# Cached attention on one core: K loaded by four heads of a batch, and the scores' matmul reading K^T in V's order of keys

## The chip, the core and the metric

The kernel runs on one core of one Trainium2 chip. A core has five engines with their own instruction streams, which wait for each other through semaphores: TensorE (PE: matmuls and transposes; its weight loads are listed as PEld), VectorE (DVE), ScalarE (ACT), GpSimd (POOL) and SyncE (SP), which here only issues loads. Sixteen DMA engines move data between the chip's memory and SBUF, the on-chip memory of 128 partitions. TensorE writes into PSUM, eight banks of 2 KB per partition. The metric is the device time of one execution in microseconds (us).

## The reference

Two independent blocks, A and B, of the same shape are computed and put side by side. With `B, Sq, D = 16, 64, 640` and `H, Sk, Dh = 32, 512, 128`, in bf16:

```python
q = (x @ wq).reshape(B, Sq, H, Dh).transpose(0, 2, 1, 3)
scores = einsum("bhqd,bhkd->bhqk", q, k_cache) * (Dh ** -0.5)
p = softmax(scores, axis=-1)
o = einsum("bhqk,bhkd->bhqd", p, v_cache)
y = o.transpose(0, 2, 1, 3).reshape(B, Sq, H * Dh) @ wo
```

The caches of K and V are by far the largest inputs: 268 MB of the 291 MB that are read. Softmax and P x V don't care in which order the 512 keys stand, as long as P's columns and V's rows stand in the same one. Both versions use that freedom.

## The kernel before

**Tiling.** Two batches of 64 queries fill 128 partitions, so a *step* `g` is one head of two batches. A *macro step* `m` is two steps, and a *period* `k` is two macro steps, that is four heads of two batches. There are 512 steps, 256 macro steps and 128 periods: four passes (a block, half of its 32 heads) of eight batch pairs of 16 heads.

**What a period does**, by the names in the plan and the lines of their emitters:

- KX (L550, PE): 32 transposes turn a loaded K tile (`kn_ring`) into K^T in PSUM banks 6 and 7, 64 keys at a time; KE (L557, DVE) copies it into `ktp_ring`. Two of each per period.
- SM (L596, PE): the scores of a step: two matmuls of 512 columns, one per batch, in the left and the right half of the array (`tile_position`), into one of four PSUM banks. Four steps per period, at its beginning.
- MX (L605, DVE) takes the negated maximum, EX (L621, ACT) the exponential into `p_ring` with the row sum, RC2 (L627, DVE) the reciprocals of two row sums, NM (L635, POOL) multiplies P by them into `pn_ring`.
- TR2 (L644, PE) transposes the two P of a macro step, and TE2 (L651, DVE) or TA2 (L656, ACT) copies the result into `pT_ring`: ACT for even macro steps, DVE for odd ones. PV2 (L666, PE) multiplies V by it, OE4 (L673, ACT) copies the result, OP2 (L681, PE) multiplies it by 512 columns of wo, and OX (L691, PE), once in four periods, by the other 128. OVP, OXP, OVF and OXF move these sums on.
- QN (L567, PE) projects queries for later heads, except near the end, and QEN (L583, ACT) copies them. QJ and QZ do so at the start. XT (L776) transposes a piece of block B's x in eight of the periods.

These steps are pipelined over periods: a period's TR2 and PV2 work on the P of the period before.

**K and V in memory.** A V load (L761) takes one batch of four heads, 512 KB: partition `p` holds keys 4p to 4p+3 of each head, in rows of 1 KB. A K load (L764) takes two heads of two batches, also 512 KB: 64 partitions per head, each with eight keys per batch, in rows of 2 KB. So K^T stands with eight groups of 64 keys, and V wants four groups of 128. The scores keep K's order. NM changes it: it reads P as `(th tl pp)` and writes `(tl pp th)`, that is two elements apart, and the transposes that follow read `pn_ring` in V's order.

**What sets the order.** Each engine's instructions are ordered by templates (`PHASES`, four of them, from periods 0, 16, 112 and 126): an entry names a kind, an offset in macro steps, a step of the macro step, and a time in the period. `build_plan` lays them out and works out the waits between engines from what each operation reads and writes.

Loads are ordered and held back by a planned clock (lines 296 to 351). `us(t)` turns a position in macro steps into planned time with `STEP_US`. A load's key is its first use less `LEAD` (K and V; V of the odd batch less `LEAD` - 1 on its pair's first use) or `WLEAD` (weights), but not before its ring slot is free: nine slots of K (`NKB`), five pairs of V (`NVP`). Loads are taken in the order of their keys; the clock starts at `START_US`, never stands before a load's key, and moves on by `DMA_US` with each. SP then holds the load until TensorE has done the last instruction planned before the clock, or, if that is earlier, before the load's first use less `BEFORE` macro steps. A lead of so many macro steps below means how far before its first use a load is let go.

Of the kernel before, what the change touches and what calls it, by code (L numbers as in the profile page):

```python
# [9 lines left out]
ALU = mybir.AluOpType  # L10
# [5 lines left out]
class Cfg:  # L16
# [6 lines left out]
    LEAD = 4.68  # L23
    WLEAD = 4.56
    STEP_US = ((8, 39.85), (32, 17.16), (256, 3.11))
    DMA_US = dict(LDK=1.40, LDV=1.44, LDWQ=1.8, LDWO=1.8, LDX=1.3, LDXR=0.5)
    START_US = -168.79
    BEFORE = 1.75
# [17 lines left out]
          ("QEZ", 0, 1, 2.19), ("QEJ", 2, 0, 2.79), ("EX", 1, 0, 3.02), ("QEN", -6, 0, 3.12), ("TA2", -2, 0, 3.58),  # L46
          ("QEZ", 0, 2, 4.2), ("EX", 1, 1, 4.36), ("XTE", 8, 0, 4.4), ("QEZ", 0, 3, 4.6), ("QEZ", 0, 4, 4.7),
          ("OVP", -3, 0, 5.0), ("QEZ", 0, 5, 5.61), ("OXP", -3, 0, 5.75), ("QEZ", 0, 6, 5.9), ("QEZ", 0, 7, 6.3)),
# [10 lines left out]
          ("QEN", -6, 0, 3.35), ("TA2", -2, 0, 3.59), ("EX", 1, 1, 4.45), ("OXP", -3, 0, 4.84), ("OVP", -3, 0, 4.86),  # L59
          ("XTE", 0, 0, 4.88)),  # L60
         (("KE", 3, 0, 0.04), ("RC2", -1, 0, 0.64), ("MX", 0, 0, 0.87), ("MX", 0, 1, 1.32), ("MX", 1, 0, 1.41),
          ("MX", 1, 1, 1.55), ("KE", 2, 0, 2.37), ("RC2", 0, 0, 3.49), ("TE2", -1, 0, 4.58), ("OXF", -3, 0, 5.55),
          ("OVF", -3, 0, 5.65)),
# [9 lines left out]
          ("OXF", -3, 0, 5.48)),  # L73
# [39 lines left out]
def build_plan(dims, cfg):  # L113
# [72 lines left out]
    def make_op(kind, m, sub, ts):  # L186
# [50 lines left out]
        if kind == "MX2":  # L237
            return mk("dve", "MX2", m, [], [bank(2 + g0 % cfg.NS), bank(2 + g1 % cfg.NS), ("negmax", r0), ("negmax", r1)],
                      ts)
        if kind == "RC4":  # L240
            rs = [g % cfg.NR for g in range(4 * k, 4 * k + 4)]
            return mk("dve", "RC4", k, [("rowsum", r) for r in rs], [("recip", r) for r in rs], ts)
        if kind == "SM":
            return mk("pe", "SM", (m, sub), [qres(2 * m + sub), ("ktp", ktslot(m))], [bank(2 + (2 * m + sub) % cfg.NS)],
                      ts)
# [222 lines left out]
def mha_kernel(nc, blocks, out, cfg=None):  # L468
# [32 lines left out]
    with contextlib.ExitStack() as es:  # L501
# [9 lines left out]
        kn_ring = sb("kn_ring", [128, NKB, 2, 8 * DH], BF16)  # L511
# [31 lines left out]
        def em_KX(e, op):  # L543
            m = op.idx
            kt_ps = [ps[:, cfg.KTB[m % 2] + hs, :].bitcast(BF16) for hs in range(2)]
            first = last = None
            for t in range(16):
                for hs in range(2):
                    r = slice(64 * hs, 64 * hs + 64)
                    last = e.transpose(kt_ps[hs][:, 64 * t:64 * t + 64], kn_ring[r, m % NKB, t // 8, t % 8 * DH:(t % 8 + 1) * DH],  # L550
                                       ident[r, r])
                    first = first or last
            return first, last
# [35 lines left out]
        def em_SM(e, op):  # L589
            m, sub = op.idx  # L590
            g = 2 * m + sub
            q = qc_ring[:, qcell[g // G // PPQ, g % SPB, g // G % PPQ // (SPB // G)], :]
            kt = ktp_ring[:, ktslot(m)].rearrange("p (hs j s) -> p hs j s", hs=2, j=2)
            first = last = None
            for j in range(2):
                ins = e.matmul(s_bank(g)[64 * j:64 * j + 64, :], q[:, 64 * j:64 * j + 64],  # L596
                               kt[:, sub, j], start=True, stop=True, tile_position=(0, 64 * j))
                first = first or ins
                last = ins
            return first, last  # L600

        def em_MX(e, op):
# [3 lines left out]
            return ins, ins  # L606

        def em_MX2(e, op):
            r, b = 2 * op.idx % NR, S_BANK0 + 2 * op.idx % NS
            ins = e.reduce_max(negmax[:, r:r + 2], ps[:, b:b + 2, :], axis=AX.X, negate=True)  # L610
            return ins, ins

        def em_RC4(e, op):
            r = 4 * op.idx % NR
            ins = e.reciprocal(recip[:, r:r + 4], rowsum[:, r:r + 4])
# [14 lines left out]
        def em_NM(e, op):  # L630
            g = op.idx
            r = g % NR
            src = p_ring[:, g % NP, :].rearrange("q (th tl pp) -> q th tl pp", th=2, tl=4)
            dst = pn_ring[:, g % NPN, :].rearrange("q (tl pp th) -> q th tl pp", tl=4, th=2)
            ins = e.tensor_scalar(dst, src, recip[:, r:r + 1], 1.0, ALU.mult, ALU.mult)  # L635
# [118 lines left out]
        def em_LDKV(e, op):  # L754
            m = op.aux
            blk, bp, grp, ps_, hh0 = step_info(2 * m)
            h0 = (ps_ % NHALF) * HH + hh0
            if op.kind == "LDV":
                h0 -= h0 % G
                src = blocks[blk][2][2 * bp + m % 2, h0:h0 + G].rearrange("g (p t) d -> p g (t d)", p=128)  # L760
                ins = e.dma_start(v_ring[:, m // 2 % NVP, m % 2], src)  # L761
# [122 lines left out]
```

## Time and profile before

| | |
|---|---|
| Median of three runs | 857.67 us (855.37 to 857.76) |
| The profiled execution | 857.66 us, its span 855.9 us |
| PE busy | 805.9 us, 94% of the span |
| DVE, ACT, POOL busy | 726.6, 633.0, 418.0 us (85, 74, 49%) |
| Moved by DMA | 297.13 MB, mean 347 GB/s |
| K loads: packets, time to landing | 65,536 of 2 KB; 6.7 us (A), 6.4 us (B) |
| V loads: packets, time to landing | 131,072 of 1 KB; 6.6 us (A), 6.3 us (B) |
| Scores' matmuls (L596) | 1,024, 137.6 us busy |
| POOL's normalization (L635) | 512 of 846 ns |
| Copies of K^T (L557) | 256 of 1,218 ns |

A profile line of a group of instructions reads: line, engine, operation, output<-input with shapes, how many; then busy time and the mean of one in ns; then the idle time of that engine just before them and what ended most of it. A line of the chain reads: start, length, engine and line, how many. The chain is followed back from the last instruction, at each step to what released it, so its shares tell which engine the end waited for. A wait line reads: who waited, for whom, us in total, how many times, the longest. Matmuls overlap, and their ends are modelled, so the spacing of groups says more than the length of one.

### The profile page before, as it was taken

Reading aid. Unit: us, or ns where it says so; the run is one execution under the profiler, and the core shown is the slowest. Engines: PE = TensorE matmul, PEld = TensorE weight load, DVE = VectorE, ACT = ScalarE, POOL = GpSimd, SP = SyncE. Lnnn points to the kernel's source line nnn. Section 1 sums busy time; section 2 is a strip of 40 time slices with the busy share of each in tenths; the row PEclk is TensorE's granted clock in tenths of the full one; section 3 lists DMA queues with packets and bytes.
Section 4 is the critical chain, followed back from the end, with each engine's and each line's share of the span. In section 5 each row is a group of like instructions: output and inputs, shape, how many; then the busy total and the mean of one; then the engine's idle time right before and its main releaser. Section 6 shows DMA issues by size and latency. Waiting matters only on the chain.

```text
span 855.9 us, 38296 instructions
## 1 busy us (share of the span) xinstructions
PE 805.9 (94%) x16953; PEld 561.8 (66%) x17084; DVE 726.6 (85%) x1184; ACT 633.0 (74%) x1450; POOL 418.0 (49%) x518
## 2 busy tenths in 40 slices
PE   5999999999999999999999899999999999999987
PEld 3566666666666766766666666666676666666665
DVE  3588888898888899898898788988888889889995
ACT  2677787787787777777777777777877867767775
POOL 0344554545544554554554445555455545446554
DMA  8999999999999999999999999999999999999993
GB/s 266 321 368 367 357 352 328 358 352 346 356 363 354 355 364 366 359 368 369 366 354 368 316 355 364 360 358 362 355 363 364 364 360 370 346 307 350 368 352 115
DMA packets 232581, 297.13 MB, mean 347 GB/s; under 512 B 14304, under 2 KB 166880, under 8 KB 232416
## 3 DMA queue, kind: packets, MB, share of 16 engines
q1 hardware_dynamic: 230112, 292.06, 100.2%
q8 instruction: 133, 2.18, 1.1%
q10 hardware_dynamic: 2304, 2.62, 0.9%
q14 instruction: 32, 0.26, 0.1%
HBM read 290.72 MB, written 2.62 MB: 343 GB/s over the span
## 4 chain that ended last, share of the span: by engine, by line
PE 81%; DMA 9%; DVE 3%; issue 3%; ACT 2%; POOL 1%; SPq 1%; POOLq 0%; ACTq 0%; DVEq 0%
PE ps L550 15%; PE ps L567 14%; PE ps L666 14%; PE ps L596 13%; PE ps L644 11%; PE ps L681 11%; DMA v_ring<-in_B_v_cache_dram 6%; PE ps L691 3%; DMA v_ring<-in_A_v_cache_dram 3%; DVE ktp_ring L557 2%; DVE negmax L605 1%; POOL pn_ring L635 1%; ACT p_ring L621 1%; DMA wq_sb<-in_A_wq_dram 1%; ACT pT_ring L656 1%
## 5 line engine op out<-in xcount | busy, mean ns | idle before, releaser
L635 POOL TENSOR_SCALAR pn_ring<-p_ring,recip 128x512 bf16<-128x512 bf16 x512 | 417.4, 846 | 429.9 <-DVE recip L627 403.2
L621 ACT ACTIVATE p_ring<-ps,negmax 128x512 bf16<-128x512 f32 x512 | 350.0, 689 | 77.5 <-DVE negmax L605 74.3
L557 DVE COPY ktp_ring<-ps 128x2048 bf16<-128x2048 bf16 x256 | 311.9, 1218 | 78.6 <-PE ps L550 78.3
L605 DVE TENSOR_REDUCE negmax<-ps 128x1 f32<-128x512 f32 x512 | 320.6, 683 | 19.7 <-PE ps L596 12.6
L550 PEld LDWEIGHTS ps<-ident,kn_ring 64*128 64x128 bf16 x8192 | 135.8, 95 | 99.2 <-issue 58.8
L550 PE MATMUL ps<-ident,kn_ring 64*128 64x64 bf16 x8192 | 167.4, 191 | 5.3 <-DVE ktp_ring L557 2.6
L673 ACT ACTIVATE oT_ring<-ps 128x512 bf16<-128x512 f32 x128 | 76.4, 597 | 123.7 <-PE ps L666 123.7
L567 PE MATMUL ps<-xT_sb,wq_sb 128*128 128x512 bf16 (+2 forms) x544 | 135.7, 376 | 26.8 <-issue 18.3
L666 PE MATMUL ps<-pT_ring,v_ring 128*128 128x64 bf16 x4096 | 142.7, 193 | 7.4 <-DMA v_ring<-in_B_v_cache_dram 4.1
L644 PEld LDWEIGHTS ps<-ident,pn_ring 128*128 128x128 bf16 x2048 | 124.9, 98 | 34.8 <-ACT p_ring L621 3.4
L644 PE MATMUL ps<-ident,pn_ring 128*128 128x128 bf16 x2048 | 137.4, 219 | 1.7 <-POOL pn_ring L635 1.2
L596 PE MATMUL ps<-ktp_ring,qc_ring 128*64 128x512 bf16 x1024 | 137.6, 387 | 1.2 <-issue 1.1
L666 PEld LDWEIGHTS ps<-pT_ring,v_ring 128*128 128x128 bf16 x4096 | 127.4, 98 | 15.9 <-DMA v_ring<-in_B_v_cache_dram 5.3
L681 PE MATMUL ps<-wo_sb,oT_ring 128*128 128x512 bf16 x497 | 132.1, 379 | 5.0 <-ACT pT_ring L656 2.5
L656 ACT ACTIVATE pT_ring<-ps 128x1024 bf16<-128x1024 bf16 x128 | 132.6, 1036 | 0.6 <-PE ps L644 0.4
L621 ACT ACTIVATION_READ_ACCUMULATOR p_ring<-ps,negmax 128x1 f32 x512 | 105.2, 206 | 0.0
L567 PEld LDWEIGHTS ps<-xT_sb,wq_sb 128*128 128x128 bf16 x660 | 54.9, 99 | 62.8 <-DMA wq_sb<-in_A_wq_dram 7.7
L651 DVE COPY pT_ring<-ps 128x1024 bf16<-128x1024 bf16 x128 | 86.3, 674 | 6.9 <-PE ps L644 6.8
L583 ACT ACTIVATE qc_ring<-ps 128x512 bf16<-128x512 f32 (+1 forms) x129 | 77.1, 597 | 14.2 <-PE ps L567 14.2
L596 PEld LDWEIGHTS ps<-ktp_ring,qc_ring 128*64 128x64 bf16 x1024 | 47.3, 109 | 37.4 <-issue 5.0
L681 PEld LDWEIGHTS ps<-wo_sb,oT_ring 128*128 128x128 bf16 x512 | 43.4, 98 | 31.8 <-ACT pT_ring L656 4.6
L627 DVE RECIPROCAL recip<-rowsum 128x2 f32<-128x2 f32 x256 | 39.9, 156 | 9.1 <-ACT p_ring L621 9.1
(16 smaller groups left out, 109.1 us busy)
## 6 DMA issues: line engine op xcount, KB each, us to landing
kn_ring<-in_A_k_cache_dram SPq DMA_DIRECT2D x128, 512.0 KB, 6.7
v_ring<-in_A_v_cache_dram SPq DMA_DIRECT2D x128, 512.0 KB, 6.6
kn_ring<-in_B_k_cache_dram SPq DMA_DIRECT2D x128, 512.0 KB, 6.4
v_ring<-in_B_v_cache_dram SPq DMA_DIRECT2D x128, 512.0 KB, 6.3
wq_sb<-in_A_wq_dram SPq DMA_DIRECT2D x8, 640.0 KB, 6.6
wo_sb<-in_A_wo_dram SPq DMA_DIRECT2D x8, 640.0 KB, 6.8
wq_sb<-in_B_wq_dram SPq DMA_DIRECT2D x8, 640.0 KB, 6.4
wo_sb<-in_B_wo_dram SPq DMA_DIRECT2D x8, 640.0 KB, 7.4
```

The lines of the kernel that those rows point to most:

```text
L550: last = e.transpose(kt_ps[hs][:, 64 * t:64 * t + 64], kn_ring[r, m % NKB, t // 8, t % 8 * DH:(t % 8 + 1) * DH], ident[r, r])
L557: ins = e.tensor_copy(ktp_ring[:, ktslot(op.idx)], ps[:, b:b + 2, :].rearrange("p b s -> p (b s)").bitcast(BF16))
L567: last = e.matmul(dst[:, col:col + n], wq_sb[:, qslot(hh // G), kt, (hh % G) * DH:(hh % G + 1) * DH], xT_sb[:, kt, lo * 128:hi * 128], sta ...
L596: ins = e.matmul(s_bank(g)[64 * j:64 * j + 64, :], q[:, 64 * j:64 * j + 64], kt[:, sub, j], start=True, stop=True, tile_position=(0, 64 * j))
L605: ins = e.reduce_max(negmax[:, r:r + 1], s_bank(g), axis=AX.X, negate=True)
L621: ins = e.activation(p_ring[:, g % NP, :], s_bank(g), ACTF.Exp, bias=negmax[:, r:r + 1], scale=1.0, accum_out=rowsum[:, r:r + 1])
L635: ins = e.tensor_scalar(dst, src, recip[:, r:r + 1], 1.0, ALU.mult, ALU.mult)
L644: ins = e.transpose(pt_flat(m)[:, (4 * sub + t) * 128:(4 * sub + t + 1) * 128], pn_ring[:, g % NPN, t * 128:(t + 1) * 128], ident[:, :])
L651: ins = e.tensor_copy(pT_ring[:, m % NT].rearrange("p s t q -> p (s t q)"), pt_flat(m))
L656: ins = e.activation(pT_ring[:, m % NT].rearrange("p s t q -> p (s t q)"), pt_flat(m), ACTF.Copy)
L666: ins = e.matmul(qo_ps[:, col:col + 64], v_ring[:, m // 2 % NVP, j, 2 * (m % 2) + sub, t * DH:(t + 1) * DH], pT_ring[:, m % NT, sub, t, 64 ...
L681: ins = e.matmul(out_ps, oT_ring[:, m // 2 % NO, 2 * (m % 2) + sub, :], wo_sb[:, wslot(ps_, hh // G), hh % G, 0:N0], start=(hh == 0), stop ...
```

## The change

K is loaded as V is: four heads of one batch per macro step, the even macro step of a period the first batch of the pair, the odd one the second. A load is still 512 KB. A head now has 32 partitions with 16 keys each, in rows of 4 KB, and `kn_ring` is declared to match. KX does the same 32 transposes; a bank of K^T now holds two heads of one batch.

So the scores of every step need both K^T tiles of their period, one per batch. SM's matmul reads its 512 keys from `ktp_ring` through `(tl, s, th)`: four neighbours in the result stand 256 elements (512 bytes) apart in `ktp_ring`, the next four begin one element further on, and so on over 32; four such blocks make the 512. The scores, and P after them, come out in V's order, and NM reads and writes without a step.

The templates have other times, and with them some instructions another place: in the middle periods OP2 and OX stand between the two TR2, and on VectorE the fourth MX stands behind KE and RC2. The planned clock's constants differ: `LEAD`, `WLEAD`, `STEP_US`, `DMA_US` of K, `START_US` and `BEFORE`. Two kinds of operation that no template uses (MX2, RC4) are gone.

```diff
-    LEAD = 4.68
-    WLEAD = 4.56
-    STEP_US = ((8, 39.85), (32, 17.16), (256, 3.11))
-    DMA_US = dict(LDK=1.40, LDV=1.44, LDWQ=1.8, LDWO=1.8, LDX=1.3, LDXR=0.5)
-    START_US = -168.79
-    BEFORE = 1.75
+    LEAD = 4.99
+    WLEAD = 4.82
+    STEP_US = ((8, 43.5), (32, 3.92), (256, 3.1))
+    DMA_US = dict(LDK=1.36, LDV=1.44, LDWQ=1.8, LDWO=1.8, LDX=1.3, LDXR=0.5)
+    START_US = -319.64
+    BEFORE = 0.68
...
         (16,
-         (("SM", 0, 0, 0.0), ("SM", 0, 1, 0.21), ("SM", 1, 0, 0.43), ("SM", 1, 1, 0.64), ("KX", 2, 0, 1.42),
-          ("QN", -6, 0, 2.07), ("TR2", -2, 0, 2.96), ("TR2", -1, 0, 3.76), ("OP2", -4, 0, 3.83),
-          ("OP2", -3, 0, 3.98), ("XT", 0, 0, 4.35), ("OX", -3, 0, 4.75), ("KX", 5, 0, 4.88), ("PV2", -2, 0, 5.52),
-          ("PV2", -1, 0, 6.09)),
+         (("SM", 0, 0, 0.0), ("SM", 0, 1, 0.21), ("SM", 1, 0, 0.43), ("SM", 1, 1, 0.64), ("KX", 2, 0, 0.92),
+          ("QN", -6, 0, 2.17), ("TR2", -2, 0, 3.28), ("OP2", -4, 0, 3.43), ("OX", -3, 0, 3.76), ("TR2", -1, 0, 4.03),
+          ("OP2", -3, 0, 4.11), ("KX", 5, 0, 4.55), ("XT", 0, 0, 4.6), ("PV2", -2, 0, 5.55), ("PV2", -1, 0, 5.79)),
...
-         (("KE", 3, 0, 0.04), ("RC2", -1, 0, 0.64), ("MX", 0, 0, 0.87), ("MX", 0, 1, 1.32), ("MX", 1, 0, 1.41),
-          ("MX", 1, 1, 1.55), ("KE", 2, 0, 2.37), ("RC2", 0, 0, 3.49), ("TE2", -1, 0, 4.58), ("OXF", -3, 0, 5.55),
-          ("OVF", -3, 0, 5.65)),
+         (("KE", 3, 0, 0.23), ("RC2", -1, 0, 0.35), ("MX", 0, 0, 0.49), ("MX", 0, 1, 1.09), ("MX", 1, 0, 2.05),
+          ("KE", 2, 0, 3.29), ("RC2", 0, 0, 4.28), ("MX", 1, 1, 4.65), ("OXF", -3, 0, 5.26), ("TE2", -1, 0, 5.66),
+          ("OVF", -3, 0, 5.81)),
...
         if kind == "SM":
-            return mk("pe", "SM", (m, sub), [qres(2 * m + sub), ("ktp", ktslot(m))], [bank(2 + (2 * m + sub) % cfg.NS)],
-                      ts)
+            return mk("pe", "SM", (m, sub), [qres(2 * m + sub), ("ktp", ktslot(2 * k)), ("ktp", ktslot(2 * k + 1))],
+                      [bank(2 + (2 * m + sub) % cfg.NS)], ts)
...
-        kn_ring = sb("kn_ring", [128, NKB, 2, 8 * DH], BF16)
+        kn_ring = sb("kn_ring", [128, NKB, 16 * DH], BF16)
...
-                    last = e.transpose(kt_ps[hs][:, 64 * t:64 * t + 64], kn_ring[r, m % NKB, t // 8, t % 8 * DH:(t % 8 + 1) * DH],
-                                       ident[r, r])
+                    last = e.transpose(kt_ps[hs][:, 64 * t:64 * t + 64], kn_ring[r, m % NKB, t * DH:(t + 1) * DH],
+                                       ident[r, 64 * hs:64 * hs + 64])
...
-            kt = ktp_ring[:, ktslot(m)].rearrange("p (hs j s) -> p hs j s", hs=2, j=2)
+            hd = 2 * (m % 2) + sub
             first = last = None
             for j in range(2):
+                kt = ktp_ring[:, ktslot(m // 2 * 2 + j)].rearrange("p (hs th tl h s) -> p hs h tl s th", hs=2, th=4, tl=4, h=2)
                 ins = e.matmul(s_bank(g)[64 * j:64 * j + 64, :], q[:, 64 * j:64 * j + 64],
-                               kt[:, sub, j], start=True, stop=True, tile_position=(0, 64 * j))
+                               kt[:, hd // 2, hd % 2], start=True, stop=True, tile_position=(0, 64 * j))
...
-            src = p_ring[:, g % NP, :].rearrange("q (th tl pp) -> q th tl pp", th=2, tl=4)
-            dst = pn_ring[:, g % NPN, :].rearrange("q (tl pp th) -> q th tl pp", tl=4, th=2)
-            ins = e.tensor_scalar(dst, src, recip[:, r:r + 1], 1.0, ALU.mult, ALU.mult)
+            ins = e.tensor_scalar(pn_ring[:, g % NPN, :], p_ring[:, g % NP, :], recip[:, r:r + 1], 1.0, ALU.mult, ALU.mult)
...
-            blk, bp, grp, ps_, hh0 = step_info(2 * m)
+            blk, bp, grp, ps_, hh0 = step_info(2 * (m - m % 2))
             h0 = (ps_ % NHALF) * HH + hh0
+            src = blocks[blk][2 if op.kind == "LDV" else 1][2 * bp + m % 2, h0:h0 + G]
             if op.kind == "LDV":
-                h0 -= h0 % G
-                src = blocks[blk][2][2 * bp + m % 2, h0:h0 + G].rearrange("g (p t) d -> p g (t d)", p=128)
-                ins = e.dma_start(v_ring[:, m // 2 % NVP, m % 2], src)
+                ins = e.dma_start(v_ring[:, m // 2 % NVP, m % 2], src.rearrange("g (p t) d -> p g (t d)", p=128))
             else:
-                src = blocks[blk][1][2 * bp:2 * bp + 2, h0:h0 + 2].rearrange("j hs (p t) d -> (hs p) j (t d)", t=8)
-                ins = e.dma_start(kn_ring[:, m % NKB], src)
+                ins = e.dma_start(kn_ring[:, m % NKB], src.rearrange("h (p t) d -> (h p) (t d)", t=16))
```

More of the change, by code (lines that the diff above doesn't have):

```diff
@@ L39 @@
         (0,
[6 rows of a table removed]
-          ("QEZ", 0, 1, 2.19), ("QEJ", 2, 0, 2.79), ("EX", 1, 0, 3.02), ("QEN", -6, 0, 3.12), ("TA2", -2, 0, 3.58),
-          ("QEZ", 0, 2, 4.2), ("EX", 1, 1, 4.36), ("XTE", 8, 0, 4.4), ("QEZ", 0, 3, 4.6), ("QEZ", 0, 4, 4.7),
-          ("OVP", -3, 0, 5.0), ("QEZ", 0, 5, 5.61), ("OXP", -3, 0, 5.75), ("QEZ", 0, 6, 5.9), ("QEZ", 0, 7, 6.3)),
[10 rows of a table removed]
-          ("QEN", -6, 0, 3.35), ("TA2", -2, 0, 3.59), ("EX", 1, 1, 4.45), ("OXP", -3, 0, 4.84), ("OVP", -3, 0, 4.86),
-          ("XTE", 0, 0, 4.88)),
-         (("KE", 3, 0, 0.04), ("RC2", -1, 0, 0.64), ("MX", 0, 0, 0.87), ("MX", 0, 1, 1.32), ("MX", 1, 0, 1.41),
-          ("MX", 1, 1, 1.55), ("KE", 2, 0, 2.37), ("RC2", 0, 0, 3.49), ("TE2", -1, 0, 4.58), ("OXF", -3, 0, 5.55),
-          ("OVF", -3, 0, 5.65)),
[9 rows of a table removed]
-          ("OXF", -3, 0, 5.48)),
[11 rows of a table removed]
[6 rows of a table added]
+          ("QEZ", 0, 1, 2.63), ("EX", 1, 0, 3.46), ("QEN", -6, 0, 3.51), ("QEZ", 0, 2, 3.61), ("TA2", -2, 0, 3.61),
+          ("ST", -33, 0, 3.79), ("QEZ", 0, 3, 4.05), ("QEZ", 0, 4, 4.15), ("QEZ", 0, 5, 4.37), ("OVP", -3, 0, 4.63),
+          ("QEZ", 0, 6, 4.91), ("OXP", -3, 0, 5.07), ("EX", 1, 1, 5.29), ("XTE", 32, 0, 6.2), ("QEZ", 0, 7, 6.29)),
+         (("KE", 3, 0, 0.16), ("RC2", -1, 0, 0.49), ("MX", 0, 0, 1.09), ("OXF", 21, 0, 1.23), ("MX", 0, 1, 1.88),
+          ("MX", 1, 0, 2.26), ("KE", 2, 0, 2.77), ("RC2", 0, 0, 3.61), ("MX", 1, 1, 4.45), ("TE2", -1, 0, 4.74),
+          ("OVF", 31, 0, 5.52)),
[6 rows of a table added]
+          ("TA2", -2, 0, 4.54), ("EX", 1, 1, 4.81), ("OVP", -3, 0, 4.97), ("XTE", 0, 0, 5.08), ("OXP", -3, 0, 5.22),
+          ("ST", -9, 0, 6.24)),
+         (("KE", 3, 0, 0.23), ("RC2", -1, 0, 0.35), ("MX", 0, 0, 0.49), ("MX", 0, 1, 1.09), ("MX", 1, 0, 2.05),
+          ("KE", 2, 0, 3.29), ("RC2", 0, 0, 4.28), ("MX", 1, 1, 4.65), ("OXF", -3, 0, 5.26), ("TE2", -1, 0, 5.66),
+          ("OVF", -3, 0, 5.81)),
[9 rows of a table added]
+          ("OVF", -3, 0, 5.88)),
[11 rows of a table added]
     )
@@ L236, in make_op @@
             return mk("act", kind, idx, [], [bank(b)] + [("qc", c_) for c_ in cells], ts, aux=cells)
-        if kind == "MX2":
-            return mk("dve", "MX2", m, [], [bank(2 + g0 % cfg.NS), bank(2 + g1 % cfg.NS), ("negmax", r0), ("negmax", r1)],
-                      ts)
-        if kind == "RC4":
-            rs = [g % cfg.NR for g in range(4 * k, 4 * k + 4)]
-            return mk("dve", "RC4", k, [("rowsum", r) for r in rs], [("recip", r) for r in rs], ts)
         if kind == "SM":
-            return mk("pe", "SM", (m, sub), [qres(2 * m + sub), ("ktp", ktslot(m))], [bank(2 + (2 * m + sub) % cfg.NS)],
-                      ts)
+            return mk("pe", "SM", (m, sub), [qres(2 * m + sub), ("ktp", ktslot(2 * k)), ("ktp", ktslot(2 * k + 1))],
+                      [bank(2 + (2 * m + sub) % cfg.NS)], ts)
         if kind == "RC2":
@@ L605, in em_MX @@
             ins = e.reduce_max(negmax[:, r:r + 1], s_bank(g), axis=AX.X, negate=True)
[L606 to L615, printed above, removed]
             return ins, ins
@@ L785, in em_XTE @@
             return ins, ins
-        emitters = dict(KX=em_KX, KE=em_KE, QJ=em_Q, QEJ=em_QE, QZ=em_Q, QEZ=em_QE, QN=em_Q, QEN=em_QE, SM=em_SM, MX=em_MX, EX=em_EX, RC2=em_RC2, MX2=em_MX2, RC4=em_RC4,
+        emitters = dict(KX=em_KX, KE=em_KE, QJ=em_Q, QEJ=em_QE, QZ=em_Q, QEZ=em_QE, QN=em_Q, QEN=em_QE, SM=em_SM, MX=em_MX, EX=em_EX, RC2=em_RC2,
                         NM=em_NM, ND=em_NM, TR2=em_TR2, TE2=em_TE2, TA2=em_TA2, PV2=em_PV2, OE4=em_OE4, OP2=em_OP2, OX=em_OX, OXH=em_OX,
```

55 rows, old and new, of the table PHASES are left out of this document.

## The prediction

> **What bounds the kernel now.** I read the engine shares first, then the DMA queues, the chain that ended last, the chain between 300 and 400 us, and the waits on loads. Four lines of the page:
>
> ```profile
> PE 805.9 (94%) x16953; PEld 561.8 (66%) x17084; DVE 726.6 (85%) x1184; ACT 633.0 (74%) x1450; POOL 418.0 (49%) x518
> ...
> q1 hardware_dynamic: 230112, 292.06, 100.2%
> ...
> PE 81%; DMA 9%; DVE 3%; issue 3%; ACT 2%; POOL 1%; SPq 1%; POOLq 0%; ACTq 0%; DVEq 0%
> ...
> L635 POOL TENSOR_SCALAR pn_ring<-p_ring,recip 128x512 bf16<-128x512 bf16 x512 | 417.4, 846 | 429.9 <-DVE recip L627 403.2
> ```
>
> TensorE carries 81% of the chain, but the load queue is full as well. POOL's normalization waits for its input about as long as it works, and is 1% of the chain. Next, the chain inside 300 to 400 us (start, length, engine and line): one period of four heads.
>
> ```profile
> 305.82 0.98 PE ps L596 x8
> 306.80 0.57 PE ps L550 x32
> 307.53 1.03 PE ps L567 x4
> 308.56 0.89 PE ps L644 x16
> 309.45 0.86 PE ps L681 x4
> 310.32 0.57 PE ps L550 x32
> 310.89 1.04 PE ps L666 x32
> 311.93 0.98 PE ps L596 x8
> ```
>
> A period is 311.93 - 305.82 = 6.11 us of TensorE with no wait for another engine. The scores (L596) take 0.98 us: four pairs, 0.245 us each. I measured every period from score group to score group: most are 6.11 us, every fourth 7.00 (L691 adds 0.89), and the eight with L776 have 0.28 more. Without the query projection (L567, absent in the last 13 periods) 5.08 would do. Of the 855.9 us, 15.6 lie before the first scores, 14.2 after the last score group starts, and 793.4 are such full periods; that leaves 32.7. Of these 12.6 belong to periods 0 to 3 (mostly extra projections), 14 to periods 4 to 112, 6 to the end, where VectorE is late. The 14 us are what a better load order could win; the waits show where half of it sits (who waited: us, times, longest):
>
> ```profile
> PEld ps L666 <- DMA v_ring<-in_B_v_cache_dram: 5.3, 9, 1.3
> ...
> PEld ps L666 <- DMA v_ring<-in_A_v_cache_dram: 2.4, 4, 1.3
> ```
>
> 7.7 us are waits of PV2 for V. The timeline of periods 67 and 68 shows two of them (start, length, then the idle time before and its releaser):
>
> ```profile
> 466.60 1.11 PE L666 MATMUL ps<-pT_ring,v_ring 128*128 128x64 bf16 x32 [1.16 <-DMA v_ring<-in_B_v_cache_dram]
> ...
> 473.79 1.11 PE L666 MATMUL ps<-pT_ring,v_ring 128*128 128x64 bf16 x32 [1.01 <-DMA v_ring<-in_B_v_cache_dram]
> ```
>
> **The change part by part.** *K's rows.* In the trace's packet records the median packet takes 46 ns for 1,024 bytes and 84 for 2,048: 38 ns per KB and 8 fixed. By that line 4,096 bytes take 160. K's 65,536 packets of 84 ns are 344 us of each of the 16 engines; 32,768 of 160 ns are 328. So 16 us, 1.9% of a queue that is 100% busy, come free. They shorten nothing while TensorE is the bound; they shorten waits for loads. From below the gain is nothing (K's queue time stays); above, it can't exceed the waits.
>
> *When loads are issued.* SP holds each load until TensorE reaches an instruction, chosen by the planner (lines 334 to 351). I worked its formula through for both sets of constants. Before, V's loads 73 and 137 are held until 1.75 half-periods (BEFORE) ahead of their PV2: 1.75 x 3.06 = 5.4 us, against a median landing of 6.3 to 6.6 us. That is about 1 us too late, which is the size of the waits in periods 37 and 69, where their PV2 runs. Loads 133 and 135 (periods 67 and 68) get 2.49 and 2.00. After, with LEAD 4.99, K at 1.36 and the lower BEFORE, loads 73, 133, 135 and 137 are released 2.30, 3.07, 2.67 and 2.32 half-periods ahead, at least 7.0 us; the mean lead of a V load in the middle of the run rises from 3.4 to 4.0. The shortest lead then exceeds the landing by 0.4 us. K's and V's rings are unchanged, and their reuse was counted. SP's issues stay 512, of 0.37 us each. If the queue got longer with the earlier issue, the landing would rise and the waits stay: at worst nothing is won. I take the 7.7 us as gone, and with them 1 us of short pauses without a named releaser beside them (0.56 and twice 0.19 us near 156 to 170 us): **-8.7 us**.
>
> *Scores with a step.* Each of the 1,024 matmuls reads its 512 columns in another order: the innermost four lie 512 bytes apart, where they were neighbours. Weights, columns and PSUM writes stay, which excludes a gain: 0 is the low end. No row shows TensorE reading its moving operand so. The only stepped stream here is POOL's own write, two elements apart: 846 ns for 512 against POOL's memsets of 102 ns (1 element) and 205 ns (128), which extrapolate to 519 ns. Taking 102 ns off each, that is 744 against 417, a factor of 1.8. On TensorE it would make 0.245 us into 0.44, +0.195 x 512 = **+100 us**, the high end, since TensorE has no cover. A nearer row: the chain's single 512-column matmul (L681) takes 0.215 us, and the score pair, two tiles each with a 512-column stream of its own, 0.245 us. So the reading side delivers two streams in nearly the time of one. That is the same engine, same memory, same operand; I therefore take 0, and keep the high end as a rival.
>
> [...]
>
> *Scores wait for both K^T tiles.* Every SM now needs the odd and the even macro step's KE. Both were already copied one period earlier: in the timeline from 414 us the later copy (KE 2) ended 4.1 us into its period, 2 us before the next scores can start. Slot 0 of ktp_ring is free for the next KE only after all four SMs, 0.5 us later, but that KE comes 1.5 us after them at the earliest. Cost 0; queued behind such a wait would be all of TensorE.
>
> *Normalization without a step.* 512 instructions on an engine that is half idle; TR2 reads the result one period later. Where POOL is on the chain (789, 805, and 843 to 848 us, some nine instructions), contiguous writes could save at most 0.33 us each, 3 us; at the low end nothing changes. I take 0, since reading and multiplying remain.
>
> *Order on the engines.* In the middle periods OP2 and OX move between the two TR2, and on VectorE the fourth maximum moves behind KE 2 and RC2. By the trace's durations the fourth maximum then ends 4.3 us into a period and TE2 at 4.95, while the PV2 that reads it starts at 5.6; the fourth EX started at 4.76 already before. Cover 0.5 to 0.6 us; with it gone the rest goes into each period. VectorE does some 5.9 of 6.11 us, so this is the thinnest cover. In the last 13 periods its chain is 3 x 0.63 + 1.13 + 0.60 + 0.60 + 0.07 + 1.12 + 0.07 = 5.48 us before and after. Cost 0, bounded by -2.5 (the delay at 737 to 757 us, where the period's plan changes, disappears) and +0.1 us per middle period, +10 us.
>
> Startup: first weights land at 7.65 us as before, and the order of the first three K copies is the same; 0, with 2 us either way.
>
> Sum: 857.66 us (the profiled execution; its span is 855.9, 1.8 lie around it; the median shown is 857.67, the same) - 8.7 = **849 us**.
>
> **The rivals.** *Half-rate scores (slower).* If the stepped read lets the array take only one of two streams at a time, a pair becomes two single matmuls, 2 x 0.215 = 0.43 us: +0.185 x 512 = 95 us. Load waits (8.7) and the end's VectorE delay (6) vanish under it: 857.7 + 95 - 15 = 938 us; with POOL's factor 943. For it: the only stepped row; against it: the pair's row. It decides from a pair of 0.262 us on, 17 ns more, where 512 x 17 ns eats the 8.7 us.
>
> *A partial loss.* Pairs 10 to 30% longer: +12.5 to +38 us, less the load waits: 861 to 887 us.
>
> *Nothing is won.* Loads issued earlier only queue longer, HBM or the queue being full (100.2%): V's waits stay and the time is 855.5 to 860. For it: busiest slices reach 370 GB/s and none more. The slice where the waits of period 67 begin moves 368. Against it: the loads that come late are those that the formula itself releases later than a landing ahead.
>
> *VectorE becomes late.* The moved maximum delays TE2 and so PV2 by 0.1 us in each of some 100 periods, +10, with the load waits gone: 858 to 870 us.
>
> **How the numbers follow.** As forecast: 0.56, own range 842 to 855 (the 8.7 us by half lost, or with POOL's 3 us and the 2.5 us won). Nothing won: 0.08. Partial loss 0.12, VectorE late 0.07, half rate 0.17. By the 0.3% (2.6 us) that a measurement of this kernel tells from no change: faster 0.56, same 0.08, slower 0.36. The range 841 to 887 holds all but the half rate, 0.83.
>
> **What the changed profile would show.** Right: L596's eight matmuls at 0.98 us in the chain, periods at 6.11 and 7.00, no PEld wait on v_ring over 0.3 us, q1's share near 98% with 32,768 packets fewer, POOL at 520 to 846 ns. Wrong: L596 at 1.1 to 1.8 us per group (stepped read), V waits with landings over 7 us (queue), or PE waits for pT_ring or ktp_ring in every period (order).

## The result, and the profile after

The changed kernel takes 1247.57 us (median of four runs, 1247.43 to 1248.33) against 856.52 us before (median of four): a ratio of 1.457 (95% interval 1.454 to 1.460). It is 391 us slower, where 849 us were forecast. The profiled execution took 1247.60 us, its span 1245.8.

The lines of the page after that answer to those shown of before:

```profile
PE 1208.2 (97%) x16942; PEld 570.7 (46%) x17084; DVE 770.9 (62%) x1184; ACT 675.2 (54%) x1450; POOL 350.4 (28%) x518
...
q1 hardware_dynamic: 197344, 292.06, 73.5%
...
PE 97%; issue 2%; ACT 0%; DMA 0%; DVE 0%; SPq 0%; ACTq 0%
PE ps L590 43%; PE ps L543 12%; PE ps L560 11%; PE ps L648 11%; PE ps L626 9%; PE ps L663 9%; PE ps L673 2%; DMA wq_sb<-in_A_wq_dram 0%; PE ps L756 0%; ACT pT_ring L638 0%; DVE ktp_ring L550 0%; ACT p_ring L605 0%; SPq L733 0%; ACT oT_ring L655 0%; DVE negmax L599 0%
...
L617 POOL TENSOR_SCALAR pn_ring<-p_ring,recip 128x512 bf16<-128x512 bf16 x512 | 349.7, 696 | 886.4 <-PE ps L626 556.0
L590 PE MATMUL ps<-ktp_ring,qc_ring 128*64 128x512 bf16 x1024 | 544.0, 1194 | 0.0
```

TensorE is now nearly the whole chain (97%), and the scores (L590; L596 before) are 43% of it, where they were 13%. Their group before read:

```profile
L596 PE MATMUL ps<-ktp_ring,qc_ring 128*64 128x512 bf16 x1024 | 137.6, 387 | 1.2 <-issue 1.1
```

The load queue, 100.2% busy before, is 73.5% busy. One period of the chain, with the PV2 just before it, from the window at 400 to 425 us:

```profile
405.24 1.04 PE ps L648 x32
406.28 4.14 PE ps L590 x8
410.42 0.57 PE ps L543 x32
410.99 0.16 issue
411.15 1.03 PE ps L560 x4
412.17 0.45 PE ps L626 x8
412.62 0.43 PE ps L663 x2
413.05 0.45 PE ps L626 x8
413.50 0.43 PE ps L663 x2
413.93 0.57 PE ps L543 x32
```

Every other step lasts as long as before. The group of eight score matmuls takes 4.14 us here instead of 0.98: a pair 1.035 us instead of 0.245, 2.0 ns for each column. Followed through the whole run, the chain's 128 such groups last between 4.07 and 4.40 us, 4.18 on average. That is 3.20 us more per period, 410 us over 128 periods. The kernel lost 391 us, so some 19 us of other time that the kernel before spent went away under the slower scores. The 7.7 us of waits for V are part of it, since no wait of TensorE for V is left; the rest was not traced to its places. The granted clock was 0.999.

### The profile page after: what moved, and what is told of

It reads as the page before. It is cut to its first block, busy times and chain, and to the rows that moved or that the text cites. A ratio compares the mean times of both kernels' runs of the same rounds, so it can differ in the third digit from the quotient of the medians.

```text
span 1245.8 us, 38217 instructions
## 1 busy us (share of the span) xinstructions
PE 1208.2 (97%) x16942; PEld 570.7 (46%) x17084; DVE 770.9 (62%) x1184; ACT 675.2 (54%) x1450; POOL 350.4 (28%) x518
## 3 DMA queue, kind: packets, MB, share of 16 engines
q1 hardware_dynamic: 197344, 292.06, 73.5%
## 4 chain that ended last, share of the span: by engine, by line
PE 97%; issue 2%; ACT 0%; DMA 0%; DVE 0%; SPq 0%; ACTq 0%
PE ps L590 43%; PE ps L543 12%; PE ps L560 11%; PE ps L648 11%; PE ps L626 9%; PE ps L663 9%; PE ps L673 2%; DMA wq_sb<-in_A_wq_dram 0%; PE ps L756 0%; ACT pT_ring L638 0%; DVE ktp_ring L550 0%; ACT p_ring L605 0%; SPq L733 0%; ACT oT_ring L655 0%; DVE negmax L599 0%
## 5 line engine op out<-in xcount | busy, mean ns | idle before, releaser
L617 POOL TENSOR_SCALAR pn_ring<-p_ring,recip 128x512 bf16<-128x512 bf16 x512 | 349.7, 696 | 886.4 <-PE ps L626 556.0
L590 PE MATMUL ps<-ktp_ring,qc_ring 128*64 128x512 bf16 x1024 | 544.0, 1194 | 0.0
L599 DVE TENSOR_REDUCE negmax<-ps 128x1 f32<-128x512 f32 x512 | 351.4, 687 | 202.6 <-PE ps L590 202.6
L590 PEld LDWEIGHTS ps<-ktp_ring,qc_ring 128*64 128x64 bf16 x1024 | 58.7, 122 | 239.4 <-issue 231.0
L626 PEld LDWEIGHTS ps<-ident,pn_ring 128*128 128x128 bf16 x2048 | 132.5, 98 | 48.3 <-issue 0.3
L626 PE MATMUL ps<-ident,pn_ring 128*128 128x128 bf16 x2048 | 153.6, 219 | 0.0
L663 PE MATMUL ps<-wo_sb,oT_ring 128*128 128x512 bf16 x470 | 143.4, 379 | 8.1 <-issue 4.6
L605 ACT ACTIVATION_READ_ACCUMULATOR p_ring<-ps,negmax 128x1 f32 x512 | 101.0, 197 | 0.0
L663 PEld LDWEIGHTS ps<-wo_sb,oT_ring 128*128 128x128 bf16 x512 | 38.3, 98 | 28.6 <-issue 23.3
```

Of the source, the lines that this page charges most:

```text
L599: ins = e.reduce_max(negmax[:, r:r + 1], s_bank(g), axis=AX.X, negate=True)
L605: ins = e.activation(p_ring[:, g % NP, :], s_bank(g), ACTF.Exp, bias=negmax[:, r:r + 1], scale=1.0, accum_out=rowsum[:, r:r + 1])
L617: ins = e.tensor_scalar(pn_ring[:, g % NPN, :], p_ring[:, g % NP, :], recip[:, r:r + 1], 1.0, ALU.mult, ALU.mult)
L626: ins = e.transpose(pt_flat(m)[:, (4 * sub + t) * 128:(4 * sub + t + 1) * 128], pn_ring[:, g % NPN, t * 128:(t + 1) * 128], ident[:, :])
L663: ins = e.matmul(out_ps, oT_ring[:, m // 2 % NO, 2 * (m % 2) + sub, :], wo_sb[:, wslot(ps_, hh // G), hh % G, 0:N0], start=(hh == 0), stop ...
```

## The experiments

**Theories.** S: a column costs about 2 ns (1.035 us over the changed kernel's 512 columns) whenever it lies in another line of 16 bytes of SBUF than the one before; at that price, an estimate, 256 changes of line come to 0.52 us a pair. D: the distance of 512 bytes, a large power of two, is at fault. Q: two stepped streams are served in turn. N: any innermost step but one element is slow. R: the loss isn't the read at all but the rows, the second K^T tile or the order.

**The change without the stepped read (e1).** K^T is read in runs of 32 neighbours, and POOL does the rest of the reordering:

```diff
-    ...rearrange("p (hs th tl h s) -> p hs h tl s th", hs=2, th=4, tl=4, h=2)
+    ...rearrange("p (hs t h s) -> p hs h t s", hs=2, t=16, h=2)
...
-            ins = e.tensor_scalar(pn_ring[:, g % NPN, :], p_ring[:, g % NP, :], recip[:, r:r + 1], 1.0, ALU.mult, ALU.mult)
+            src = p_ring[:, g % NP, :].rearrange("q (th tl s) -> q th tl s", th=4, tl=4)
+            dst = pn_ring[:, g % NPN, :].rearrange("q (tl s th) -> q th tl s", th=4, tl=4)
+            ins = e.tensor_scalar(dst, src, recip[:, r:r + 1], 1.0, ALU.mult, ALU.mult)
```

> Everything of the change is kept but the stepped read: the scores read K^T in runs of 32 neighbours, and the normalization on POOL brings P into V's order, writing four elements apart. If the whole loss is the stepped read: groups of eight score matmuls back at 0.98 us, periods at 6.11 us, 849 us as the prediction's sum had it without that term (842 to 855). If the loss is the 4 KB rows, the wait for both K^T tiles or the new order of instructions: near 1247 us. If POOL's wider step hurts: 846 ns rises above 1,200 ns and waits of TR2 for pn_ring appear, 860 us and more.

Measured: 898.12 us, ratio 1.049 (1.047 to 1.052). Groups of this kernel:

```profile
L619 POOL TENSOR_SCALAR pn_ring<-p_ring,recip 128x512 bf16<-128x512 bf16 x512 | 680.6, 1415 | 204.5 <-DVE recip L611 183.2 <-PE ps L628 20.3
L590 PE MATMUL ps<-ktp_ring,qc_ring 128*64 128x512 bf16 x1024 | 136.7, 387 | 0.7 <-issue 0.7
```

The scores are back at 136.7 us (137.6 before), so R falls: rows, both K^T tiles and order together are not the 391 us. The 42 us that remain go with POOL: writing four elements apart takes it 1,415 ns, against 846 at two and 696 without a step, and it is 29% of this kernel's chain. The kernel with a step of 4 bytes further down (e11) bears this out. It has the rows, both tiles and the order too, but no step on POOL, and takes 857.48 us. With the planned clock's old constants (e2):

> As the kernel with runs of 32, but the loads' planned clock has the constants of before. If the earlier release of V's loads is what takes its waits away: the waits of PV2 for V stay near 7 us and the time is 856 to 858 us. If the cheaper 4 KB rows do it by themselves: 849 to 851 us.

Measured: 901.23 us, ratio 1.054 (1.052 to 1.056). POOL's longer time hides what the expectation asked for; the waits of PV2 for V were 3.3 us there, and none with the new constants.

**What makes the read slow.** Six kernels (e5, e6, e7, e8, e11 and e12, with their expectations below in this order) change only the order in which the score matmul reads, for instance e6:

```diff
-    ...rearrange("p (hs th tl h s) -> p hs h tl s th", hs=2, th=4, tl=4, h=2)   [:, hd // 2, hd % 2]
+    ...rearrange("p (i o) -> p o i", o=8)[:, 2 * hd:2 * hd + 2]                  # step of 16 bytes
```

> Of each pair of score matmuls only the one of the second batch reads with the step of 512 bytes; the first reads 512 neighbours (so the first batch's scores have their keys in another order, and its output is not the reference's). If each stream is slowed by itself: the pair still takes 1.03 us, time near 1247 us. If two stepped streams are served in turn and one costs half: pair 0.52 us, 843 + 512 x 0.275 = 984 us.

> Score matmuls read 512 columns with an innermost step of 8 elements, 16 bytes (the keys are mixed over heads, so the output is not the reference's). If a column costs 2.0 ns whenever it lies in another 16-byte line than the one before: pair 1.03 us, 1247 us. If the 512 bytes, a large power of two, are at fault: pair 0.245 us, 843 to 855 us.

> Innermost step of 4 elements, 8 bytes: two columns in each 16-byte line (keys mixed over heads, output not the reference's). [...] If any innermost step other than one element is slow: 1.03 us, 1247 us.

> Score matmuls read runs of two neighbours, the next run 128 bytes on (keys out of V's order, output not the reference's). [...] If what counts is the distance or the number of jumps of 128 bytes and more: between 0.52 and 1.03 us.

> Score matmuls read 512 columns with a step of two elements, 4 bytes, so four columns in each 16-byte line (keys mixed over heads, output not the reference's). If a line costs 1.8 to 2.0 ns however it is used: 128 lines x 1.85 = 0.237 us, under the 0.245 us of a pair, so no loss and 843 to 855 us. If the cost of a column falls in proportion to the step only by halves (1.81 ns at 16 bytes, 0.93 at 8, then 0.47): also 0.245 us. If any step but one element costs something: groups over 1.05 us and more than 858 us.

> Score matmuls read with an innermost step of 128 bytes over 16 places, then one element further on (keys out of V's order, output not the reference's). Each column lies in another line, as at 16 bytes (1.81 ns per column) and in the changed kernel's pattern at 512 bytes (2.02). If only the change of line counts: 0.925 us per pair, near 1185 us. If the distance adds: between 0.925 and 1.035 us per pair, 1185 to 1247 us.

A group of eight score matmuls in the chain of the kernels with steps of 16 bytes, 8 bytes, runs of two, and steps of 4 and 128 bytes, in this order, and last of the kernel where one stream of two is stepped (seven of its eight records are in the chain):

```profile
406.16 3.70 PE ps L590 x8
```

```profile
404.13 1.91 PE ps L590 x8
```

```profile
404.36 1.90 PE ps L590 x8
```

```profile
407.44 1.02 PE ps L590 x8
```

```profile
408.50 3.74 PE ps L590 x8
```

```profile
409.43 3.57 PE ps L594 x7
```

| Read of 512 columns | changes of a 16-byte line | group, us | pair, us | ns per line | time, us |
|---|---|---|---|---|---|
| neighbours (before) | 64 | 0.98 | 0.245 | | 856.5 |
| runs of 32 (e1) | 64 | | as before | | |
| step of 4 bytes (e11) | 128 | 1.02 | 0.255 | | 857.5 |
| step of 8 bytes (e7) | 256 | 1.91 | 0.478 | 1.87 | 955.9 |
| runs of two, 128 bytes on (e8) | 256 | 1.90 | 0.475 | 1.86 | 955.9 |
| step of 16 bytes (e6) | 512 | 3.70 | 0.925 | 1.81 | 1184.9 |
| step of 128 bytes (e12) | 512 | 3.74 | 0.935 | 1.83 | 1189.5 |
| 512 bytes (the change) | 512 | 4.14 (mean 4.18) | 1.035 | 2.02 | 1247.6 |
| 512 bytes, one stream of two (e5) | 512 | 3.57 | 0.89 | 1.74 | 1194.7 |

(Times of e5 to e8, e11 and e12 are of one run each. The groups of these six repeat to within 0.1 us in nearly all periods of their runs. The pairs of before and of e11 are near the 0.215 us that one matmul of 512 neighbours takes in the chain before, so no price per line can be read from them. The granted clock of e5 was 0.977 over its run, that of the other kernels of the table 0.996 or more; what of e5's time goes with that was not separated.)

S holds: the cost follows the number of times that the read moves to another line of 16 bytes, at 1.7 to 2.0 ns each, and all but hides once four columns in a row share a line (0.255 us a pair against 0.245). The size of the line can be read from the rows: from a step of 8 bytes to one of 16 the cost doubles, and from 16 to 128 it stays. It isn't the number of different lines that counts, since the changed kernel's 512 columns lie in only 64 of them and come back to each eight times. D falls: 16 bytes cost nearly as much as 512. N falls with the step of 4 bytes. Q falls: one stepped stream beside a contiguous one holds the pair for 0.89 us, more than half of 1.035; each stream is slowed by itself. The changed kernel's own pattern costs 0.1 us more than the other two with 512 changes of line, and why was not separated. In one stream alone (e5) it costs no more than they do, 1.74 ns, and all groups last 3.57 to 3.59 us; only with two such streams side by side does the group grow, and vary between 4.07 and 4.40 us.

**Other places for the order of keys.** ScalarE's exponential writes P with the step (e9), or POOL reads with it (e10):

```diff
+            dst = p_ring[:, g % NP, :].rearrange("q (tl s th) -> q th tl s", th=4, tl=4)    # e9, in EX
+            src = s_bank(g).rearrange("q (th tl s) -> q th tl s", th=4, tl=4)
...
+            src = p_ring[:, g % NP, :].rearrange("q (th tl s) -> q tl s th", th=4, tl=4)    # e10, in NM
+            dst = pn_ring[:, g % NPN, :].rearrange("q (tl s th) -> q tl s th", th=4, tl=4)
```

> The change with the order of keys made in another place: scores read runs of 32 neighbours, EX on ScalarE writes P four elements apart into V's order, the normalization on POOL has no step (696 ns). If ScalarE's stepped write costs nothing: groups of scores 0.98 us, periods 6.11 us, no engine late, 845 to 852 us, the sum of the prediction without the stepped read. If it slows ScalarE as the step of four slowed POOL (1,415 against 696 ns): 0.7 us more for each of four EX in a period, ScalarE at 7.8 us per period, near 1,000 us.

> Scores read runs of 32 neighbours; the normalization on POOL writes neighbours and reads with a step, 256 bytes innermost. If only POOL's stepped write is slow: about 700 to 1,050 ns each, POOL at 2.8 to 4.2 us per period, 845 to 855 us. If a stepped read costs it as much as the stepped write: 1,415 ns or more and 898 us or more.

Measured: 1029.72 us (ratio 1.204, 1.202 to 1.206) and 863.01 us (1.009, 1.007 to 1.011). The groups of the first and of the second:

```profile
L607 ACT ACTIVATE p_ring<-ps,negmax 128x512 bf16<-128x512 f32 x512 | 669.5, 1411 | 71.6 <-POOL pn_ring L619 56.1 <-DVE negmax L599 15.0
```

```profile
L619 POOL TENSOR_SCALAR pn_ring<-p_ring,recip 128x512 bf16<-128x512 bf16 x512 | 585.3, 1155 | 267.0 <-DVE recip L611 235.7 <-PE ps L628 31.2
```

So a step of four elements, which rows of 4 KB bring with them, costs 3.2 us per period on TensorE, 0.72 us for each of four instructions on ScalarE or POOL as a write, and 0.46 as POOL's read. None of the places tried carries it for nothing. The step of two that the kernel before has costs POOL 0.15 us, under cover.

**Where the 8.7 us of the forecast went.** Two kernels put the new constants (e3), and then the new constants and templates (e4), on the kernel before:

> The kernel before with nothing but the new constants of the planned clock; K in 2 KB rows, old templates. If the earlier release suffices: waits for V gone, 849 to 852 us. If the queue is full with 2 KB rows and earlier loads only queue longer: landing times over 7 us, 855 to 859 us.

> The kernel before with the new constants and the new templates; K in 2 KB rows, contiguous score reads, the normalization's step of two. If the order of instructions costs nothing, as predicted: the same as with the new constants alone within 2 us. If the moved maximum makes VectorE late: 5 to 13 us more than with the new constants alone.

Measured: 852.51 us (ratio 0.9966, 0.9950 to 0.9981) and 855.24 us (0.9992, 0.9976 to 1.0009). With the constants alone the waits for V fell from 7.7 to 2.3 us:

```profile
PEld ps L666 <- DMA v_ring<-in_A_v_cache_dram: 1.3, 3, 0.6
PEld ps L666 <- DMA v_ring<-in_B_v_cache_dram: 1.0, 2, 0.6
```

With the new templates none are left, and yet the time is that of before. The view of `out_sb` in that kernel shows a wait that the kernel before doesn't have:

```profile
its engine sat idle before it (us, times) until:
  DMA out_dram<-out_sb: 8.2, 5
```

The templates move the output's store (ST) from offset -5 at 0.76 us to -9 at 6.24 us. That is four macro steps and 5.5 us, nearly three periods later: in this trace the first store is issued 21.2 us after the first sum begins to write `out_sb`, in that of the next kernel 2.5 us. VectorE's next sum needs `out_sb` and waits until the store has landed (5.5 us after its issue, the median), and VectorE, 85% busy before, has little to spare. The store's old places in the new templates (e13):

```diff
-          ("ST", -9, 0, 6.24)),
+          ("ST", -5, 0, 0.76)),                        # and so in the other three templates
```

> The kernel before with new constants and new templates, but the output's store (ST) in its old places. If the late store, for which VectorE's next sum waited 8.2 us, is what the new order costs: those waits vanish and the time is 851 to 853 us, as with the new constants alone. If the order of VectorE or TensorE costs: 855 us as with the whole new order.

Measured: 853.07 us, ratio 0.9971 (0.9956 to 0.9987), and no such wait. The median is 2.2 us under e4 and within 1 us of the constants alone, so the late store is what the new order costs. The amount is known only roughly, since single runs of the two kernels overlap (852.4 to 858.8 and 851.0 to 856.3 us). The last three give the 4 KB rows the old templates (e14 and e15), and run the new constants alone again beside them (e16):

> K in 4 KB rows, new constants, old templates; scores read runs of 32, and the normalization reads with a step (1,155 ns). If the rows win what the queue's packet times say and POOL's step stays under cover: 848 to 851 us. If POOL's longer normalization is late for TR2: 855 to 863 us. If the rows win nothing: 852 to 854 us, as with the new constants alone.

> K in 4 KB rows, new constants, old templates; scores read with a step of 4 bytes (0.255 us per pair; keys mixed over heads, output not the reference's), normalization without a step (696 ns). Against the new constants alone, the scores cost 512 x 0.01 = 5 us more. If the rows win V's last waits (2.3 us) and no more: 854 to 857 us. If they win more: under 853 us.

> The kernel before with the new constants alone, again, as the one to compare with on this chip: 851 to 854 us, 0.3 to 0.4% under before.

Measured: 858.86 us (1.0032, 1.0016 to 1.0048), 852.97 us (0.9964, 0.9948 to 0.9981) and 852.37 us (0.9966, 0.9949 to 0.9983). Of e14, the waits of TR2 for POOL; of e15, the wait for V that is left, and the queue:

```profile
PEld ps L629 <- POOL pn_ring L620: 15.5, 17, 1.8
```

```profile
PEld ps L649 <- DMA v_ring<-in_A_v_cache_dram: 0.3, 1, 0.3
```

```profile
q1 hardware_dynamic: 197344, 292.06, 98.4%
```

In e14 POOL's 1,157 ns are late for TR2. In e15 the waits for V are 0.3 us, the queue is 98.4% busy instead of 100.9% (e16), and a plain period lasts 6.15 us instead of 6.11, 5 us over the run, for the step of 4 bytes. It still ties with the constants alone, so by this sum rows and step-free normalization together are worth about 5 us; which of the two was not separated. The best kernel with the reference's result that was run is the old one with the new constants, 0.34% under before.

## Why the prediction was wrong, step by step

- **Scores with a step: the step that failed.** The prediction took 0 and put the high end at +100 us; it is +410 (3.20 us in each of 128 periods). The row it trusted, a pair in 0.245 us against a single matmul in 0.215, shows two streams in nearly the time of one while neighbours are read. It says nothing of reads that change line with every column. The high end was a guess from another engine's write, over a baseline extrapolated from two memsets (519 ns, where a line through the two rows gives 516; measured without a step 696). So both ends came from rows that didn't show the thing, the range ended below even its own half-rate rival, and the probability on a loss of that kind, 0.17, was too small for a cost with no row and no cover.
- **The half-rate rival** had the place right (L590 longer, everything else equal, V's waits gone) and the size wrong: 938 us against 1247. It assumed two streams taking turns; e5 shows each stream slowed by itself, to 0.89 us for a pair with only one stepped stream.
- **A price for changes of line.** No row of before shows one; e6, e7, e8, e11 and e12 do. With one column per line of 16 bytes the pair took 0.925 us at a step of 16 bytes, with two 0.478 us, twice its time of 0.245, and with four 0.255 us.
- **K's rows: right in the queue.** 4,096 bytes were put at 160 ns; the packet records after give a median of 159. The queue's share in e15 is 2.5 points under that of e16; 1.9% was forecast.
- **When loads are issued: right in kind, mis-sized.** The new constants took 5.4 of the 7.7 us of V's waits on the old rows, all but 0.3 with the new; but the time fell by 3.4 us (e16), not 8.7. V's loads still land late at times there (2.3 us of waits), and where the rest of the forecast gain went was not traced.
- **Order on the engines: wrong.** It was put at 0 with VectorE's maximum as the risk. The moved maximum cost nothing that can be seen (e13, which has it, takes 853.07 us against 852.51 and 852.37 without). The store, which the prediction didn't name among the moved steps, cost 2 to 3 us (855.24 us in e4). And of the two OP2 of a period only one moved between the two TR2, as the chain after shows.
- **Both K^T tiles: right.** No wait of the scores for a K^T tile appears, not in the changed kernel and not in e11 or e15, which run at the pace of before. **Normalization without a step:** 846 to 696 ns, 0.15 us each, inside the 0 to 0.33 given, and off the chain.

## What to carry to other kernels

A reordering of keys had to be paid in every place that was tried, and TensorE's moving operand was the dearest: 391 us, with TensorE 81% of the chain before, against 7, 42 and 174 us in the other places (e10, e1, e9). Four bf16 columns in a row from one 16-byte line took 0.255 us a pair, two 0.478, one 0.925 to 1.035: where TensorE is the bound, let at least four come from one line. An engine that looks half idle isn't free either: POOL, 49% busy before, went with 42 us more when it took the step of four as a write (e1), and with 6 to 7 us more when it took it as a read (e10 against before, e14 against e16). When an access pattern has no row in the profile and its engine no cover, the range has to reach to several times the time that the engine takes now, not to a fraction of it: here a group of scores went from 0.98 to 4.18 us. And among moved instructions, look at the stores too: `out_sb`, written again, had to wait for its store, 8.2 us in e4.

## What the runs showed of the hardware

Each change to another 16-byte line costs TensorE's moving read 1.7 ns in one stream beside a contiguous one (e5), and 1.8 to 2.0 ns in each of two stepped streams side by side (e6, e7, e8, e12 and the changed kernel). ScalarE and POOL, different engines with different work, write 512 bf16 with a step of 8 bytes in nearly the same time, 1,411 (e9) and 1,415 ns (e1), 2.76 ns an element, about twice what they take for neighbours (689 and 696); with a step of 4 bytes POOL takes 846 ns (before).
